# Decode attention beside an MLP: TensorE's loop over single (group, batch) pairs instead of two

## The chip, the cores and the metric

The kernel runs on one core of a Trainium2 chip. The metric is the device time of the program in microseconds (us). Every engine of the core runs its own instruction stream: TensorE (PE, with its weight loads shown as PEld), VectorE (DVE), ScalarE (ACT), GpSimd (POOL) and SyncE (SP), which here only issues transfers. They wait for each other by semaphores.

## The reference, cut to what matters

```python
def _A_ref(x, k_cache, v_cache, wq, wo):      # B=8, Sq=1, D=640, 32 heads, Sk=4096, Dh=128
    q = (x @ wq).reshape(B, Sq, Hq, Dh).transpose(0, 2, 1, 3)
    scores = jnp.einsum("bhqd,bhkd->bhqk", q, k_cache) * (Dh ** -0.5)
    o = jnp.einsum("bhqk,bhkd->bhqd", softmax(scores), v_cache)
    return o.transpose(0, 2, 1, 3).reshape(B, Sq, Hq * Dh) @ wo

def _B_ref(x, w1, b1, w2, b2):                # F=1728
    h = gelu(layernorm(x) @ w1 + b1)
    return h @ w2 + b2

xn = layernorm(x)
return x + _A_ref(xn, k_cache, v_cache, wq, wo) + _B_ref(xn, w1, b1, w2, b2)
```

All inputs are bfloat16. The K and V caches are 268 MB each, so nearly all that the kernel reads is cache.

## The kernel before, in words

The work is cut into 32 pairs i of a group of eight heads and one batch element. A pair's K is one transfer of 8.4 MB: partition (head, p) holds 256 consecutive keys of one head, 64 KB in a row. V has the same layout. K alternates between two slots (`kslot`), V has one slot (`VS`). SP issues in the order K(1), V(0), K(2), V(1), and so on; K(i) waits until K(i-2) has been worked off (`("kt", i-2)`, the last transposes and scores on TensorE's side, and `("km", i-2)`, the last VectorE chunk), and V(i) waits for the value product of pair i-1 (`("pv", i-1)`). An issue that waits holds up the ones behind it.

The scores of a pair come from two engines. TensorE takes `jp_of(i)` of the 256 keys of each partition, 128 for pair 0 and 80 for the others: `pe_T` transposes eight key blocks into one PSUM bank, `act_T` copies them to SBUF on ScalarE, `pe_QK` multiplies them with the query. VectorE takes the other keys in three chunks (`dve_chunk`: multiply by the broadcast query, add halves, reduce) and selects TensorE's scores with a mask (`dve_sel`). `dve_max` makes the maxima, `act_exp` eight exponentials, `pe_RS` the row sums, `pe_PV` the 256 products with V, `act_O` and `o_norm` the normalised output. `fin_wo` multiplies it with wo, in four parts (`WO_CUT`); wo lies in a K slot and its first two parts are multiplied between the products of pairs 30 and 31, the other two after that of pair 31. V of pair 31 comes in four pieces (`V_CUT`), each with a semaphore, and the product waits for each.

Nothing of this is scheduled by a compiler. Each step is given a position (`at(pos, fn, ...)`), the steps are recorded in the order of their positions, and each engine's list is replayed. Positions are 100 per pair: a pair's transposes and scores stand at 0 to 44, its exponentials at 90, its value product at 150, behind the transposes of the next pair. Only for pair 0 the exponentials stand at 145:

```python
at(o + 90 if i else o + Q + 45, act_exp, i)
at(o + Q + 48, pe_RS, i)
at(o + Q + 50, pe_PV, i)
```

To keep the program short, TensorE, VectorE and ScalarE replay the 15 equal stretches of two pairs from pair 2 on as a loop (`_replay_loop`), in which the value that a wait compares with grows with the loop's register. Pairs 0 and 1, the last product and wo are straight code around the loop. TensorE's loop head is put on the first slot of a block of instructions (`head_slot`).

The head of the program loads wq, w1, w2 and K(0), computes the queries and the whole MLP on TensorE (`pe_q`, `pe_mlp1`, `pe_mlp2`), and lets SP issue K(1) and V(0) after that.

Of the kernel before, what the change touches and what calls it, by code (L numbers as in the profile page):

```python
# [8 lines left out]
BF = mybir.dt.bfloat16  # L9
# [57 lines left out]

class _Dma:
# [26 lines left out]
def _emit(e, call, wait=None):  # L95
    name, a, k, inc = call
    if name == "wait_ge":
        e.wait_ge(a[0], a[1] if wait is None else wait, **k)
        return
    inst = getattr(e, name)(*a, **k)  # L100
    if inc is not None:
        inst.then_inc(*inc)
# [7 lines left out]
def _same(x):  # L110
    if hasattr(x, "ap") and hasattr(x, "offset"):
        return (x.tensor.name, x.offset, str(x.ap), str(x.dtype))
    return str(x)


def _replay_loop(e, calls, a, b, n, slot=None):

    size = (b - a) // n
    assert size * n == b - a and n >= 2
    _replay(e, calls[:a])  # L120
    body = calls[a:a + size]
    grow = []
    for j, (name, args, kw, inc) in enumerate(body):
        step = 0
        for r in range(1, n):
            name_r, args_r, kw_r, inc_r = calls[a + r * size + j]
            assert name_r == name and inc_r == inc and sorted(kw_r) == sorted(kw), (j, name, name_r)
            if name == "wait_ge":
                assert args_r[0] is args[0]
                if r == 1:  # L130
                    step = args_r[1] - args[1]
                assert args_r[1] == args[1] + r * step and args[1] > 0 and step >= 0, (j, args, args_r)
            else:
                assert [_same(x) for x in args_r] == [_same(x) for x in args], (j, name)
                assert [_same(kw_r[x]) for x in sorted(kw)] == [_same(kw[x]) for x in sorted(kw)], (j, name)
        grow.append(step)
    head = {} if slot is None else {"head_slot": {e.engine: slot}}
    with e.bass.Fori(0, n, engines=OrderedEngineSet([e.engine]), **head) as r:
        for call, step in zip(body, grow):
            _emit(e, call, call[1][1] + r * step if step else None)  # L140
    _replay(e, calls[b:])


def bass_parallel_sum__gqa_block_cached__mixer_channel_mlp__decode_kernel(
# [33 lines left out]
    V_CUT = (0, 96, 176, 232, 256)  # L178

    def jp_of(i):  # L180
        return 128 if i == 0 else 80
# [16 lines left out]
    with ExitStack() as es:  # L198
# [41 lines left out]
        qrep_sb = sb("qrep_sb", [P, 2, HS, HP], BF)  # L240
# [12 lines left out]
        rs_sb = sb("rs_sb", [P, 2, HS], F32)  # L253
        ri_sb = sb("ri_sb", [P, 2, HS], F32)
        ones_f = sb("ones_f", [P, P], F32)
        res_sb = sb("res_sb", [P, DC * B], BF)
# [12 lines left out]
        RS_ps = CH_ps[:, 384:384 + 2 * HS].rearrange("p (s h) -> p s h", h=HS)  # L269
# [3 lines left out]
        pe, dve, act, sp, pool = (_Eng(sem(f"{n}_s")) for n in ("pe", "dve", "act", "sp", "pool"))  # L273
        ld_s = [_Dma(sem(f"ld_s{s}")) for s in range(3)]
        ld_x, ld_b1, ld_b2, ld_wq, ld_w1, ld_w2a, ld_w2b, st_o = (
            _Dma(sem(n)) for n in ("ld_x", "ld_b1", "ld_b2", "ld_wq", "ld_w1", "ld_w2a", "ld_w2b", "st_o"))
        ld_vl = [_Dma(sem(f"ld_vl{q}")) for q in range(len(V_CUT) - 1)]
# [14 lines left out]
        def load_k(i):  # L292
            s = kslot(i)
            if i >= 2:
                sp.wait(tk[("kt", i - 2)], tk[("km", i - 2)])
            elif s == KB:
                sp.wait(tk["mlp"])
            tk[("k", i)] = ld_s[s].sig(sp.dma_start(tile[s], cache_src(A_k_cache, i)))

        def load_v(i):  # L300
            sp.wait(tk["mlp"] if i == 0 else tk[("pv", i - 1)])
            if i < NQ - 1:
                tk[("v", i)] = [ld_s[VS].sig(sp.dma_start(tile[VS], cache_src(A_v_cache, i)))]
                return
            tk[("v", i)] = [
                d.sig(sp.dma_start(tile[VS][:, lo:hi, :], cache_src(A_v_cache, i)[:, lo:hi, :]))
                for d, lo, hi in zip(ld_vl, V_CUT[:-1], V_CUT[1:])]

# [6 lines left out]
        def consts_pool():  # L315
            pool.iota(iota_h, [[-HP, HS]], base=0, channel_multiplier=1)
            tk["iota"] = pool.sig(pool.iota(iota_i, [[1, P]], base=0, channel_multiplier=-1))
            pool.memset(zeros_sb, 0.0)
            pool.memset(ones_sb, 1.0)
            pool.memset(mx_sb[:, :], 0.0)  # L320
            pool.memset(mb_sb[:, :], 0.0)
            tk["consts"] = pool.sig(pool.memset(ones_f[:, :], 1.0))
# [98 lines left out]
        def qrep(i):  # L421
            hq, b = divmod(i, B)
            s = i % 2
            pool.wait(tk["q"], tk.get(("qb_pe", i - 2)), tk.get(("qkl", i - 2)))
            tk[("qrep", i)] = pool.sig(pool.tensor_copy(
                qrep_sb[:, s, :, :],
                qT_sb[:, hq * HS:(hq + 1) * HS, b][:, :, None].to_broadcast([P, HS, HP])))

        def pe_qbc(i):
            pe.wait(tk[("qrep", i)], tk["id"])  # L430
            QBB.use(pe)
            tk[("qb_pe", i)] = QBB.used(pe, pe.sig(pe.matmul(
                QB_ps[:, 0:DH], qrep_sb[:, i % 2, :, :].rearrange("p h r -> p (h r)"),
                ident_bf[:, :], start=True, stop=True)))

        def act_qbc(i):
            act.wait(tk.get(("ym", i - 2)))
            QBB.use(act)
            tk[("qb", i)] = QBB.used(act, act.sig(act.activation(
                qbc_sb[:, i % 2, :], QB_ps[:, 0:DH], ACT.Copy)))  # L440

        def pe_T(i, t):
            n = group0[i] + t
            k = n % 2
            s = kslot(i)
            j0 = NKEY - jp_of(i) + t * TPB
            pe.wait(tk["id"], tk[("k", i)])
            TRB[k].use(pe)
            for jj in range(TPB):
                last = pe.transpose(TR_ps[:, k, jj * P:(jj + 1) * P], tile[s][:, j0 + jj, :], ident_bf[:, :])  # L450
            tk[("kt", i)] = TRB[k].used(pe, pe.sig(last))
# [13 lines left out]
        def pe_QK(i, t):  # L465
            n = group0[i] + t
            f = int(t >= halves(i)[1])
            t0 = halves(i)[f]
            pe.wait(tk[("ev", n)], tk[("qrep", i)])
            if t == t0:  # L470
                SBK[f].use(pe)
            for jj in range(TPB):
                c0 = ((t - t0) * TPB + jj) * HS
                last = pe.matmul(S_ps[:, f, c0:c0 + HS], KT_sb[:, n % NS, jj, :],
                                 qrep_sb[:, i % 2, :, 0], start=True, stop=True)
            tk[("qk", n)] = SBK[f].used(pe, pe.sig(last))
            tk[("qkl", i)] = tk[("qk", n)]

        def dve_chunk(i, c):
# [4 lines left out]
            dve.wait(tk[("k", i)], tk[("qb", i)])  # L484
# [40 lines left out]
        def act_exp(i):  # L525
            s = i % 2
            act.wait(tk[("nb", i)], tk.get(("pv", i - 1)), tk.get(("rs", i - 2)))
            for h in range(HS):
                last = act.activation(P_sb[:, h, :], Sd_sb[:, s, :], ACT.Exp, bias=NB_sb[:, s, h:h + 1],
                                      scale=SCALE, accum_out=rs_sb[:, s, h:h + 1])  # L530
            tk[("exp", i)] = act.sig(last)

        def pe_RS(i):
            s = i % 2
            pe.wait(tk[("exp", i)], tk["consts"])
            CHB.use(pe)
            tk[("rs", i)] = CHB.used(pe, pe.sig(pe.matmul(
                RS_ps[:, s, :], ones_f[:, :], rs_sb[:, s, :], start=True, stop=True)))

        def dve_rinv(i):  # L540
            CHB.use(dve)
            if i == NQ - 1:
                dve.wait(tk[("on", i - 2)])
            tk[("ri", i)] = CHB.used(dve, dve.sig(dve.reciprocal(ri_sb[:, i % 2, :], RS_ps[:, i % 2, :])))

        def pe_PV(i):
            PVB.use(pe)
            pe.wait(tk[("exp", i)])
            for j in range(NKEY):
                if j == 0 or (i == NQ - 1 and j in V_CUT):  # L550
                    pe.wait(tk[("v", i)][V_CUT.index(j)])
                last = pe.matmul(PV_ps[:, 0:HS], tile[VS][:, j, :], P_sb[:, :, j],
                                 start=(j == 0), stop=(j == NKEY - 1))
            tk[("pv", i)] = PVB.used(pe, pe.sig(last))

        def act_O(i):
            PVB.use(act)
            tk[("oU", i)] = PVB.used(act, act.sig(act.activation(oU_sb[:, i % 2, :], PV_ps[:, 0:HS], ACT.Copy)))

        def o_norm(i):  # L560
            hq, b = divmod(i, B)
# [59 lines left out]
        for i in range(NQ):  # L621
# [5 lines left out]
            at(o - 60, qrep, i)  # L627
# [14 lines left out]
            at(o + 90 if i else o + Q + 45, act_exp, i)  # L642
# [5 lines left out]
            at(o + Q + 75, o_norm, i)  # L648
        o = NQ * Q
# [4 lines left out]
        engs = {"pe": pe, "dve": dve, "act": act}  # L654
        marks = {n: [] for n in engs}
        for m in range(LOOPN + 1):
            for n in engs:
                at((LOOP0 + 2 * m) * Q - 12, lambda n=n: marks[n].append(len(engs[n].calls)))

# [3 lines left out]
        def replay(e, n):  # L663
            m = marks[n]
            assert len({y - x for x, y in zip(m, m[1:])}) == 1, (n, m)
            _replay_loop(e, engs[n].calls, m[0], m[-1], LOOPN, 0 if n == "pe" else None)
# [6 lines left out]
        def _(e):  # L673
            replay(e, "pe")
# [40 lines left out]
```

## Time and profile before

| what | value |
| --- | --- |
| median of 3 runs | 1288.85 us (1288.84 to 1289.09) |
| profiled execution | 1288.79 us, span 1287.0 us |
| bytes moved, mean rate | 552.15 MB, 429 GB/s |
| busy share of the span | PE 46%, PEld 41%, DVE 84%, ACT 36%, POOL 6% |
| mean granted TensorE clock | 0.619 |

The span runs from the first to the last instruction of the profiled execution; the rest of its own time lies around the span. Times inside the profile are counted from the span's start. A row of the timeline gives start, duration, engine, line, operation, result and operands with their shapes, the count, and in brackets the idle time before it with what ended it. A row of the chain gives start, duration and what the chain rests on there. A row of the windows gives the stretch, its length, the busy time and count of PE, PEld, DVE, ACT and POOL, the granted clock, the DMA share and GB/s. Nearly every instruction has line 100, since the recording layer issues them all there; tiles tell them apart: `TR_ps` transposed keys, `KT_sb` their copy, `S_ps` scores, `P_sb` exponentials, `CH_ps` row sums, `PV_ps` the value product, `ACC_ps` the sum of the outputs.

### The profile page before, as it was taken

How to read it: one execution, taken by the hardware profiler on the slowest of the kernel's cores; microseconds unless marked ns; L12 is line 12 of the kernel's file. 1: busy time of each engine (PE TensorE's matmuls, PEld its weight loads, DVE VectorE, ACT ScalarE, POOL GpSimd, SP SyncE). 2: the span in 40 equal slices, each digit the busy share in tenths (PEclk: the TensorE clock that was granted, in tenths of full speed). 3: DMA queues.
4: the chain of work that ended last, by engine and by line, in shares of the span. 5: the costliest groups of instructions: out<-in, count | busy, mean ns of one | idle time of the engine just before them, and what ended most of it. 6: DMA issues, size and time to landing. Idle time of an engine off the chain costs nothing.

```text
span 1287.0 us, 31562 instructions
## 1 busy us (share of the span) xinstructions
PE 590.6 (46%) x14000; PEld 527.9 (41%) x14000; DVE 1082.2 (84%) x662; ACT 468.4 (36%) x909; POOL 72.0 (6%) x74
## 2 busy tenths in 40 slices
PE   4454543553443453443453443553543553543554
PEld 4353443443443453443443443442433452433443
DVE  1599988988888988888988888988888988888982
ACT  1444432244432244432344432344432344422341
POOL 0001000000000000000000000000000000000000
PEclk9966555666655666656666655666556666656665
DMA  9999999999999999999999999999999999999998
GB/s 400 445 424 433 425 439 434 424 440 438 426 436 442 426 428 444 432 426 440 436 426 434 444 426 428 446 430 424 442 436 426 434 444 426 430 446 428 424 407 327
DMA packets 14413, 552.15 MB, mean 429 GB/s; under 512 B 1260, under 2 KB 5429, under 8 KB 5558
## 3 DMA queue, kind: packets, MB, share of 16 engines
q1 hardware_dynamic: 14320, 551.79, 99.5%
q8 instruction: 18, 0.29, 0.1%
q10 hardware_dynamic: 70, 0.03, 0.0%
q14 instruction: 5, 0.04, 0.0%
HBM read 551.80 MB, written 0.01 MB: 429 GB/s over the span
## 4 chain that ended last, share of the span: by engine, by line
DMA 78%; PE 17%; ACT 1%; DVE 1%; issue 1%; SPq 0%; another core or an unknown queue 0%; ACTq 0%
DMA S_sb<-in_A_v_cache_dram 75%; PE PV_ps L100 17%; DMA S_sb<-in_A_k_cache_dram 3%; ACT KT_sb L100 1%; DVE S_sb L100 1%; ACT P_sb L100 0%; DVE Sd_sb L100 0%; SPq L100 0%; PE TR_ps L100 0%; PE ACC_ps L100 0%; PE QB_ps L100 0%; PE S_ps L100 0%; DVE S_ps L100 0%; PE CH_ps L100 0%
## 5 line engine op out<-in xcount | busy, mean ns | idle before, releaser
L100 DVE TENSOR_TENSOR S_sb<-S_sb,qbc_sb 128x7552 bf16<-128x7552 bf16 (+3 forms) x96 | 385.6, 4016 | 149.1 <-DMA S_sb<-in_A_k_cache_dram 149.0
L100 PE MATMUL TR_ps<-ident_bf,S_sb 128*128 128x128 bf16 (+1 forms) x2618 | 260.5, 264 | 373.4 <-DMA S_sb<-in_A_k_cache_dram 365.9
L100 DVE TENSOR_REDUCE Sd_sb<-S_sb 128x59 f32<-128x3776 bf16 (+3 forms) x96 | 387.0, 4031 | 3.3
L100 PEld LDWEIGHTS TR_ps<-ident_bf,S_sb 128*128 128x128 bf16 (+1 forms) x2618 | 203.5, 119 | 379.3 <-DMA S_sb<-in_A_k_cache_dram 371.8
L100 ACT ACTIVATE KT_sb<-TR_ps 128x1024 bf16<-128x1024 bf16 x326 | 321.1, 1022 | 81.2 <-PE TR_ps L100 79.0
L100 PE MATMUL PV_ps<-P_sb,S_sb 128*128 128x8 bf16 x8192 | 225.1, 175 | 218.4 <-DMA S_sb<-in_A_v_cache_dram 208.2
L100 PEld LDWEIGHTS PV_ps<-P_sb,S_sb 128*128 128x128 bf16 x8192 | 221.5, 103 | 221.8 <-DMA S_sb<-in_A_v_cache_dram 211.5
L100 ACT ACTIVATE P_sb<-Sd_sb,NB_sb 128x256 bf16<-128x256 f32 x256 | 126.3, 494 | 230.3 <-DVE NB_sb L100 230.3
L100 DVE TENSOR_TENSOR S_sb<-S_sb 128x3776 bf16<-128x3776 bf16 (+3 forms) x96 | 201.4, 2098 | 3.3
L100 ACT ACTIVATE oU_sb<-PV_ps 128x8 f32<-128x8 f32 x31 | 5.5, 177 | 450.2 <-PE PV_ps L100 450.2
L100 PE MATMUL S_ps<-qrep_sb,KT_sb 128*128 128x8 bf16 x2608 | 123.8, 177 | 73.3 <-ACT KT_sb L100 61.5
L100 PEld LDWEIGHTS S_ps<-qrep_sb,KT_sb 128*128 128x128 bf16 x2608 | 95.2, 101 | 124.8 <-ACT KT_sb L100 87.3
L100 POOL TENSOR_TENSOR oT_sb<-oU_sb,ri_sb 128x8 bf16<-128x8 f32 x31 | 64.3, 2074 | 1122.3 <-ACT oU_sb L100 1089.4
L100 ACT ACTIVATION_READ_ACCUMULATOR P_sb<-Sd_sb,NB_sb 128x1 f32 x256 | 47.7, 186 | 0.0
L100 DVE TENSOR_REDUCE Sd_sb<-S_ps 128x40 f32<-128x320 f32 (+1 forms) x64 | 31.9, 498 | 2.2
L100 DVE TENSOR_TENSOR S_ps<-S_ps,mask_sb 128x320 f32<-128x320 f32 (+1 forms) x64 | 31.8, 496 | 1.5 <-PE S_ps L100 1.5
L100 PE MATMUL CH_ps<-rs_sb,ones_f 128*128 128x8 f32 x64 | 12.4, 266 | 12.1 <-ACT P_sb L100 12.1
L100 PEld LDWEIGHTS CH_ps<-rs_sb,ones_f 128*128 128x128 f32 x64 | 10.2, 201 | 12.3 <-ACT P_sb L100 12.3
L100 DVE TENSOR_REDUCE mx_sb<-Sd_sb 128x1 f32<-128x256 f32 x32 | 13.4, 420 | 1.1
L100 PE MATMUL CH_ps<-S_sb 128*128 128x8 bf16 (+1 forms) x244 | 12.0, 181 | 5.0 <-DMA S_sb<-in_A_wq_dram 4.4
L100 PEld LDWEIGHTS CH_ps<-S_sb 128*128 128x128 bf16 (+1 forms) x244 | 11.4, 120 | 5.7 <-DMA S_sb<-in_A_wq_dram 4.4
L100 ACT ACTIVATE qbc_sb<-QB_ps 128x128 bf16<-128x128 f32 x32 | 8.9, 277 | 11.8 <-PE QB_ps L100 9.9
(41 smaller groups left out, 87.7 us busy)
## 6 DMA issues: line engine op xcount, KB each, us to landing
S_sb<-in_A_wq_dram SPq DMA_DIRECT2D x1, 5120.0 KB, 15.2
S_sb<-in_A_v_cache_dram SPq DMA_DIRECT2D x1, 3072.0 KB, 12.8
S_sb<-in_A_wo_dram SPq DMA_DIRECT2D x1, 2560.0 KB, 32.4
S_sb<-in_A_v_cache_dram SPq DMA_DIRECT2D x1, 2560.0 KB, 20.0
S_sb<-in_B_w_dram SPq DMA_DIRECT2D x1, 2160.0 KB, 19.9
S_sb<-in_B_w_dram SPq DMA_DIRECT2D x1, 2080.0 KB, 25.7
S_sb<-in_A_v_cache_dram SPq DMA_DIRECT2D x1, 1792.0 KB, 23.8
S_sb<-in_A_wo_dram SPq DMA_DIRECT2D x1, 1280.0 KB, 35.6
```

Of the source, the lines that this page charges most:

```text
L100: inst = getattr(e, name)(*a, **k)
```

## The change

- TensorE's loop has 32 turns of one pair. Turn r holds the transposes and scores of pair r and the row sums and value product of pair r-1. Since K's slot alternates, each transpose takes its address from the loop's register (`_Slot`), which adds one register instruction a transpose.
- The last turn has no pair 32. A branch on the register (`If_lt`, `If_eq`) runs in its place the first two parts of wo, whose instructions stand in the loop's body and are jumped over in the other turns. The last value product is the loop's own; its waits for V's pieces stand in all turns and compare with 1 or, in the last turn, 17, and GpSimd sets these semaphores to 1 at the start. Behind the loop stand only the last two parts of wo and the store. `head_slot` is gone.
- So that all turns are alike: pair 0 takes 80 keys on TensorE like the others, its exponentials stand at 90 like the others (ahead of pair 1's evictions on ScalarE), some steps get a stand-in for pair -1 or 32, the repeated query and the row sums have one buffer instead of two, and TensorE waits for K through GpSimd (`k_ready`: a wait for the load, then a small memset that signals).
- K(0) comes in two transfers, keys 0 to 116 and 117 to 255; VectorE's first two chunks of pair 0 wait for the first.
- VectorE's and ScalarE's loops stay.

```diff
+class _Slot:
+    def __init__(self, slots, i, lo, n):
+        self.slots, self.i, self.lo, self.n = slots, i, lo, n
+    def at(self, i):
+        return self.slots[:, i % 2, self.lo:self.lo + self.n]
...
+def _replay_pe(e, calls, head, mid, end, late):
+    n = len(head)
+    first = [calls[a:b] for a, b in zip(head, mid)]
+    second = [calls[a:b] for a, b in zip(mid, head[1:] + [end])]
+    g1, g2 = _steps(first[:-1]), _steps([[c for c in t if not _late(c, late)] for t in second])
+    _replay(e, calls[:head[0]])
+    with e.bass.Fori(1, n + 1, engines=OrderedEngineSet([e.engine])) as r:
+        reg = e.to_reg(r)
+        with e.If_lt(reg, n):
+            for call, step in zip(first[0], g1):
+                _emit(e, call, call[1][1] + (r - 1) * step if step else None, r)
+        with e.If_eq(reg, n):
+            _replay(e, first[-1])
+        g = iter(g2)
+        for call in second[0]:
+            if _late(call, late):
+                e.wait_ge(call[1][0], (r >> (n.bit_length() - 1)) * 16 + 1)
+            else:
+                step = next(g)
+                _emit(e, call, call[1][1] + (r - 1) * step if step else None)
+    _replay(e, calls[end:])
...
+    K_CUT = (0, 117, 256)
     def jp_of(i):
-        return 128 if i == 0 else 80
+        return 80
...
-            tk[("k", i)] = ld_s[s].sig(sp.dma_start(tile[s], cache_src(A_k_cache, i)))
+            if i == 0:
+                lo, hi = K_CUT[0:2]
+                tk["k0"] = ld_k0.sig(sp.dma_start(tile[s][:, lo:hi, :], cache_src(A_k_cache, i)[:, lo:hi, :]))
+            lo, hi = K_CUT[1:3] if i == 0 else (0, NKEY)
+            tk[("k", i)] = ld_s[s].sig(sp.dma_start(tile[s][:, lo:hi, :], cache_src(A_k_cache, i)[:, lo:hi, :]))
...
+        def k_ready(i):
+            pool.wait(tk[("k", i)])
+            tk[("kr", i)] = pool.sig(pool.memset(kr_sb[:, :], 0.0))
...
         def pe_T(i, t):
-            pe.wait(tk["id"], tk[("k", i)])
+            pe.wait(tk["id"], tk[("kr", i)])
...
-                last = pe.transpose(TR_ps[:, k, jj * P:(jj + 1) * P], tile[s][:, j0 + jj, :], ident_bf[:, :])
+                last = pe.transpose(TR_ps[:, k, jj * P:(jj + 1) * P], _Slot(S_sb, i, (j0 + jj) * DH, DH),
+                                    ident_bf[:, :])
...
-            dve.wait(tk[("k", i)], tk[("qb", i)])
+            dve.wait(tk["k0"] if i == 0 and c < 2 else tk[("k", i)], tk[("qb", i)])
...
-            act.wait(tk[("nb", i)], tk.get(("pv", i - 1)), tk.get(("rs", i - 2)))
+            act.wait(tk[("nb", i)], tk.get(("pv", i - 1)))
...
-                if j == 0 or (i == NQ - 1 and j in V_CUT):
-                    pe.wait(tk[("v", i)][V_CUT.index(j)])
+                if j == 0:
+                    pe.wait(tk[("v", i)][0])
+                elif j in V_CUT:
+                    pe.wait_ge(ld_vl[V_CUT.index(j) - 1].sem, 1)
...
-            at(o - 60, qrep, i)
+            at(o - 52, qrep, i)
+            at(o - 2, k_ready, i)
...
-            at(o + 90 if i else o + Q + 45, act_exp, i)
+            at(o + 90, act_exp, i)
...
+        for i in range(1, NQ + 1):
+            at(i * Q - 12, mark, head)
+            at(i * Q + 47, mark, mid)
+        at(NQ * Q + 79, mark, end)
```

## The prediction

> **What bounds the kernel now.** I read the page's busy slices and queue table first, then the chain of waits in order of time, SP's timeline, TensorE's timeline at the head, and the windows of the tail.
>
> ```profile
> DMA  9999999999999999999999999999999999999998
> q1 hardware_dynamic: 14320, 551.79, 99.5%
> q8 instruction: 18, 0.29, 0.1%
> 1177.96 31.64 DMA S_sb<-in_A_v_cache_dram
> 1209.65 7.00 PE PV_ps L100 x256
> 1216.67 31.65 DMA S_sb<-in_A_v_cache_dram
> 1248.37 7.01 PE PV_ps L100 x256
> ```
>
> The DMA row is full from the second slice to the last but one: transfers bound the kernel. The chain looks like a loop of V load (31.6 us) and value product (7.0 us), 38.7 us a pair, but that is how the chain is followed back. One pair's K and V are 16.78 MB, and at the 433 to 434 GB/s that the windows give for a pair this is 38.7 us alone. V's 31.6 us hold 12.3 us of queueing behind K, so the product may end about 12 us later before an engine of the DMA runs dry; K is issued 25 us ahead.
>
> ```profile
> 74.06 0.33 SPq L100 DMA_DIRECT2D S_sb<-in_A_k_cache_dram  x1
> 96.21 0.33 SPq L100 DMA_DIRECT2D S_sb<-in_A_v_cache_dram  x1
> 85.79 6.39 PE L100 MATMUL PV_ps<-P_sb,S_sb 128*128 128x8 bf16 x233 [1.56 <-DMA S_sb<-in_A_v_cache_dram]
> 95.42 0.76 PE L100 MATMUL PV_ps<-P_sb,S_sb 128*128 128x8 bf16 x23 [3.24 <-issue]
> 128.61 3.58 PE L100 MATMUL PV_ps<-P_sb,S_sb 128*128 128x8 bf16 x128 [0.23 <-issue]
> 135.63 1.31 PE L100 MATMUL PV_ps<-P_sb,S_sb 128*128 128x8 bf16 x43 [3.43 <-issue]
> 1278.00:1280.00 2.00, 0.12 (x5) 0.02 (x1) 0.00 (x0) 0.00 (x0) 0.00 (x0) 0.50 0.75 287
> 1280.00:1282.00 2.00, 1.69 (x57) 1.60 (x58) 0.00 (x0) 0.00 (x0) 0.00 (x0) 0.50 0.39 141
> 1282.00:1284.00 2.00, 1.62 (x56) 1.56 (x57) 0.19 (x1) 0.00 (x0) 0.00 (x0) 0.50 0.07 20
> ```
>
> The products with "issue" in front stand still for up to 3.4 us with nothing to wait for, at boundaries 128 matmuls apart. A matmul is two instructions, so a block is 256, and each stop ends 1.3 us after a packet of the instruction queue (16,384 bytes, 18 in all). From one new block to the next such a burst needs 7.0 us (128.61 to 135.63), of which it computes 3.6.
>
> The last three rows show a ragged end: the DMA share falls from 0.75 to 0.07 over 4 us. The trace's packet records say why. A 64 KB packet takes 2.42 us and there are 16 such chains, one per engine. An instruction packet holds its engine 1.0 to 1.1 us, and the data packet behind it takes 2.9 instead of 2.42: about 1.5 us lost on that engine, which nothing gives back while all queues are full. The 16 completion marks of a load lie 0.5 us apart at 24.5 us, 2.0 at 65, 3.5 from 122 on. Fifteen of the 18 packets fall between 20 and 177 us, in turn on eight engines, so most of these carry two. At 1260, 1273 and 1281 us three more follow. The last V piece has its first mark at 1276.8 and its last at 1281.5 us, and the last piece of wo 1278.5 and 1283.16: the slowest engine is 4.7 us behind the fastest at the end.
>
> **The tail, changed.** In the built programs TensorE's code falls from 4,586 to 2,278 instructions; the loop is 1,190 instead of 1,709 and has only 85 behind it. With the block positions that the stall at product 233 fixes (63 instructions ahead of the program), the loop lies in blocks 4 to 8 and the tail ends in block 9. That leaves 8 instruction packets instead of 18, one to each of the eight engines, and none before the last V piece. If nothing else moved, engines with two packets would be one packet's 1.5 us earlier and those with three 3.0: the last V mark of a one-packet engine is 1280.0 - 1.5 = 1278.5 us against 1281.5, and the last mark of wo 1281.66 - 1.5 = 1280.2 against 1283.16. Behind them stand 24 products (0.8), the normalisation (0.2), 40 matmuls (1.2) and the store, unchanged. The loop's exit branch (76 ns) hides under the 0.34 us between the last product and the first wo matmul. Gain 3.0 us.
>
> **The steady turns.** 80 address computations a turn, one per transposed K block. TensorE's 75 fused register operations in the trace take 40 ns: 3.2 us a turn in its sequencer. K's score work of a pair now takes 11.8 us (609.77 to 621.56) and V lands at 629.1, so 7.5 us are free before the product moves at all, and 12.3 more before the DMA starves. Branches back take 208 ns, once a turn. GpSimd's new wait for K(i) has the next repeat of the query and the next normalisation queued behind it, and TensorE's transposes wait for its memset (0.1 us); the normalisation ahead of it is over 10 us before K lands (597.72 + 2.10 against 609.8), and the two behind it are needed only after this pair's scores and the next product, so K's landing still rules. The single buffers of query and row sums are free by then for the same reason. Nothing here; without the cover each turn would pay 3.2 us or more.
>
> **The head.** Three edits act here. K(0) in two pieces: VectorE starts with 117 keys, 139/256 of 19.4 us or 10.5 us earlier, at 36.4 instead of 46.97. It now has 176 keys rather than 128, by chunk rows of pair 2's kind 10.1, 10.3 and 10.3 us plus 1.9 for the selected scores. Chunks 0 and 1 end at 56.9, the second selection waits for TensorE until 59.2, chunk 2 ends at 70.6 (before: 74.0), and K(2), which waits for it, is issued 3.5 us earlier, under a queue that lasts to 83 us: worth nothing. 128 extra packets cost 8 ns each, eight to an engine: below 0.1 us.
>
> The exponentials of pair 0 now stand ahead of pair 1's evictions on ScalarE (before, behind them). They wait for the maxima (72.1) and take 4.0, so evictions that ran from 67.0 start at 76.1. TensorE's scores of pair 1 then end about 11.1 us later, at 87.2 (pair 2's row: 113.97 to 125.07, also started behind exponentials); before they ended at 78.7. Behind them on TensorE wait the row sums, V(0)'s product and, on SP, V(1)'s load. All of it is new code in the first turn. Block 6 is asked for when block 5 is entered, at the sixth transposed group (80.7), and is there 7.0 us later, 87.7. Take 88.0 for the jump over the wo branch into block 6; two more blocks at 7.0 us each and 102 products at 27 ns give 104.8 us for the end of V(0)'s product; it was 96.2.
>
> K(2)'s marks, the last work in the queues, run from 102.64 to 104.62. V(1) issued at 104.9 finds engines idle. The first packet comes 1.05 us after an issue (0.73 to 1.78 at the start), the last engine's up to 1.2 us after that. So all engines restart 3.3 to 4.4 us behind the fastest engine's schedule of before, and stay there, nearly level, since later instruction packets fall into the gap. I take 3.8.
>
> **Sum.** The slowest engine ends 3.8 instead of 4.7 us behind the same fastest one: 0.9 us gained, not 3.0. The profiled execution was 1288.79 us around a span of 1287.0, and the median is 1288.85: 1288.79 - 0.9 = 1287.9. The three runs agree within 0.25 us; 0.2% (2.6 us) is taken as no change.
>
> [...]
>
> **Rivals.** *No gap.* If a new block came in 5 us rather than 7, V(0)'s product ends at 100.8 and V(1) reaches the queues by 102: no engine waits, and the 3.0 us remain, 1285.8. For it: part of the 7 us is waiting for data packets of 2.42 us. Against it: three bursts of 6.7 to 7.0 us, and a cold branch of 7.02 us at 95.67.
>
> *Slower: the register addresses set the pace at the head.* No row shows a weight load whose address is in a register. Bounds: nothing, since 40 ns hide beside 76 ns a transpose, to about 85 ns each, the distance of a register operation from the load behind it (611.908 to 611.993), all of it in the open. A score group, 1.1 us now, would then take up to 1.8; pair 1's scores end at 94. From 1.2 us a group on the kernel is slower than before (the restart 0.9 us later). At 1.55 they end at 91.7, V(1) restarts 3.7 us later, 7.5 behind: 1288.8 + 2.8 = 1291.6. I took no delay, since TensorE's queue is fed ahead elsewhere; this end sets the range's top.
>
> *Every turn fetches its code again.* 31 turns of 5 packets on eight engines, 1.5 us each: 29 us, 1318. The loop of before, longer, ran from 177 to 1260 us without one packet, which speaks against it. [...]
>
> *The split and the shorter code do nothing at the end,* because the last V piece waits for something else: 1288.8. Against it are the marks.
>
> **How the numbers follow.** Small gap 0.45 (1286.4 to 1289.4, by 1.5 us either way of its restart); no gap 0.20; slow register addresses 0.20, of which 0.13 beyond 2.6 us; fetching every turn 0.05; nothing 0.10. Faster by over 0.2% is the second case, 0.20. Slower is 0.13 + 0.05 = 0.18. The rest, 0.62, is within. The range goes from the no-gap case (1285.7) to most of the slow one (1291.2); outside lie refetching, the worst addresses and some of the no-gap case.
>
> **What would show it.** Right: 8 packets on the instruction queue, none after 110 us before the last V piece; V(1) issued at 104 to 106 us with the DMA share below 0.9 around 104 to 106; the marks of a load nearly level from there on; 38.7 us a pair. Wrong: packets in every turn, V(1) before 102 with the share at 1.0 (no gap), or scores of pair 1 ending after 91 us.

## The result, and the profile after

The median after is 1290.34 us (22 runs, 1289.61 to 1293.13), against 1288.75 us before (22 runs): a ratio of 1.0018 with a 95% interval of 1.0011 to 1.0024. The change makes the kernel slower by 1.6 us, where 0.9 us of gain was forecast. The size is under the 0.2% that the prediction takes as no change, but the sign is clear: the fastest run after is slower than the slowest before. The profiled execution is 1290.35 us, 1.56 above that of before, so the two profiles show the difference that is to be explained. (The 22 times fall in two groups, 13 at 1289.6 to 1290.5 and 9 at 1292.0 to 1293.1; the profile belongs to the lower one.)

The page after, lines on the span, the DMA's busy slices and the queues:

```profile
span 1288.5 us, 34287 instructions
DMA  9998999999999999999999999999999999999998
q1 hardware_dynamic: 14464, 551.79, 99.4%
q8 instruction: 9, 0.15, 0.0%
```

The same bytes take 1.5 us longer, and the fourth slice (97 to 129 us) is no longer full. The instruction queue has 9 packets instead of 18: by the packet records at 21.6, 28.7, 51.9, 61.8, 86.0, 93.0, 100.5, 104.2 and, behind all the loads, 1285.4 us. The chain of waits, start, duration and what it rests on:

```profile
105.94 21.78 DMA S_sb<-in_A_v_cache_dram
127.77 7.04 PE PV_ps L111 x256
134.82 31.63 DMA S_sb<-in_A_v_cache_dram
166.50 7.04 PE PV_ps L111 x256
```

V(1)'s load takes 21.8 us here where the next one takes 31.6: there was no queue in front of it. From the second row on a pair takes 38.7 us, as before. TensorE's and SP's timelines at the head:

```profile
88.79 0.39 PE L111 MATMUL S_ps<-qrep_sb,KT_sb 128*128 128x8 bf16 x8 [0.86 <-ACT KT_sb L111]
89.96 0.90 PE L111 MATMUL PV_ps<-P_sb,S_sb 128*128 128x8 bf16 x28
95.49 3.57 PE L111 MATMUL PV_ps<-P_sb,S_sb 128*128 128x8 bf16 x128 [4.63 <-issue]
103.07 2.84 PE L111 MATMUL PV_ps<-P_sb,S_sb 128*128 128x8 bf16 x100 [4.01 <-issue]
105.94 0.33 SPq L111 DMA_DIRECT2D S_sb<-in_A_v_cache_dram  x1
```

The scores of pair 1 end at 89.18, V(0)'s product stands still twice for code, 4.63 and 4.01 us (each stop ends 1.4 to 1.5 us after a packet of the instruction queue does), and V(1) is issued at 105.94; before, at 96.21. The windows, DMA share in the last column but one, at the head and at the end:

```profile
102.00:104.00 2.00, 0.93 (x34) 0.93 (x35) 2.00 (x1) 0.00 (x0) 0.00 (x0) 0.50 0.15 66
104.00:106.00 2.00, 1.91 (x72) 1.82 (x69) 1.86 (x5) 0.05 (x1) 0.00 (x0) 0.50 0.03 8
1280.00:1282.00 2.00, 0.84 (x31) 0.85 (x32) 0.00 (x0) 0.00 (x0) 0.00 (x0) 0.50 0.97 390
1282.00:1284.00 2.00, 1.63 (x55) 1.45 (x52) 0.06 (x1) 0.00 (x0) 0.00 (x0) 0.50 0.77 266
1284.00:1286.00 2.00, 1.42 (x41) 1.26 (x41) 0.34 (x2) 0.00 (x0) 0.00 (x0) 0.50 0.04 10
```

For nearly 4 us next to nothing moves. At the end the share falls from 0.97 to 0.04 over two windows, where before it sank through 0.75, 0.39 and 0.07: the engines now end together. Their common end is late, though: V(1)'s 16 completion marks lie at 126.87 to 127.41 us (before 122.0 to 125.45), wo's last at 1284.15 (before 1283.16). What stands behind the loads is as before: the last V piece releases its 24 products at 1283.04 (before 1281.98), the normalisation and wo's last products follow, then the store's issue at 1286.42 (before 1285.30) and ScalarE's end.

### The profile page after: what moved, and what is told of

The parts are those of the page before. It is cut to its first block, busy times and chain, and to the rows that moved or that the text cites. A ratio compares the mean times of both kernels' runs of the same rounds, so it can differ in the third digit from the quotient of the medians.

```text
span 1288.5 us, 34287 instructions
## 1 busy us (share of the span) xinstructions
PE 672.9 (52%) x13904; PEld 573.5 (45%) x13904; DVE 1089.4 (85%) x663; ACT 475.4 (37%) x906; POOL 77.4 (6%) x107
## 4 chain that ended last, share of the span: by engine, by line
DMA 78%; PE 18%; ACT 1%; DVE 1%; issue 1%; SPq 0%; POOL 0%; ACTq 0%; DVEq 0%
DMA S_sb<-in_A_v_cache_dram 75%; PE PV_ps L111 17%; DMA S_sb<-in_A_k_cache_dram 3%; PE TR_ps L111 1%; ACT KT_sb L111 1%; DVE S_sb L111 0%; DVE Sd_sb L111 0%; PE S_ps L111 0%; ACT P_sb L111 0%; SPq L111 0%; PE ACC_ps L111 0%; PE CH_ps L111 0%; DVE S_ps L111 0%; DVE mx_sb L111 0%; PE QB_ps L111 0%
## 5 line engine op out<-in xcount | busy, mean ns | idle before, releaser
L111 PE MATMUL TR_ps<-ident_bf,S_sb 128*128 128x128 bf16 (+1 forms) x2570 | 339.9, 276 | 381.9 <-POOL kr_sb L111 367.4
L111 DVE TENSOR_TENSOR S_sb<-S_sb,qbc_sb 128x7552 bf16<-128x7552 bf16 (+1 forms) x96 | 388.8, 4050 | 143.7 <-DMA S_sb<-in_A_k_cache_dram 143.5
L111 PEld LDWEIGHTS TR_ps<-ident_bf,S_sb 128*128 (+2 forms) x2570 | 244.0, 103 | 439.4 <-issue 364.6
L111 DVE TENSOR_REDUCE Sd_sb<-S_sb 128x59 f32<-128x3776 bf16 (+1 forms) x96 | 390.2, 4065 | 3.3
L111 ACT ACTIVATE KT_sb<-TR_ps 128x1024 bf16<-128x1024 bf16 x320 | 326.9, 1023 | 124.1 <-PE TR_ps L111 112.6
L111 DVE TENSOR_TENSOR S_sb<-S_sb 128x3776 bf16<-128x3776 bf16 (+1 forms) x96 | 202.9, 2114 | 3.3
L111 PE MATMUL S_ps<-qrep_sb,KT_sb 128*128 128x8 bf16 x2560 | 122.0, 177 | 41.8 <-ACT KT_sb L111 38.3
L111 POOL TENSOR_TENSOR oT_sb<-oU_sb,ri_sb 128x8 bf16<-128x8 f32 x31 | 60.5, 1953 | 397.8 <-ACT oU_sb L111 381.2
L111 POOL COPY qrep_sb<-qT_sb 128x128 bf16<-128x128 bf16 x32 | 12.8, 399 | 461.1 <-PE S_ps L111 441.4
L111 DVE TENSOR_REDUCE Sd_sb<-S_ps 128x40 f32<-128x320 f32 x64 | 31.5, 492 | 2.2
L111 DVE TENSOR_TENSOR S_ps<-S_ps,mask_sb 128x320 f32<-128x320 f32 x64 | 31.4, 490 | 1.7 <-PE S_ps L111 1.7
```

## The experiments

The theory: the time is that of the DMA engine that is last; all engines restart with V(1) after the gap, so the time follows V(1)'s issue; V(1) is late through cold code in the loop's first turn. Cold is a block of 256 instructions that TensorE runs for the first time, warm one that has run. The profile before shows both. Counted in TensorE's records, back from the stop at product 233 and, in the loop, on from its first instruction at 102.75 us (the stops at 135.62 and 172.47 are its instructions 768 and 1,536), each of the 15 blocks entered first between 18 and 173 us is followed by one packet of 16,384 bytes, 2.8 to 5.0 us later (95.42 by that at 100.23, 128.61 by that at 132.99, 135.62 by that at 140.64); products that reach the next block sooner stand still, for up to 3.43 us. From 177 to 1260 us, where the loop's code has run, there is no such packet. The rivals: the steady turns or the slower transposes cost the time, instruction packets are worth nothing, or the loop as such makes the gap.

**A first turn that only branches.** TensorE's loop starts at 0; the turn with register 0 skips every section, so that the blocks are touched in idle time.

```diff
-    with e.bass.Fori(1, n + 1, engines=OrderedEngineSet([e.engine])) as r:
+    with e.bass.Fori(0, n + 1, engines=OrderedEngineSet([e.engine])) as r:
...
+        u = (r + (n - 1)) & (n - 1)          # in place of r - 1 in the waits
+        with e.If_ne(reg, 0):                # around both sections of the turn
```

> The changed kernel with one more turn of TensorE's loop ahead of the others, in which every section is jumped over: its branches only touch blocks 5, 6 and 8 of the code while TensorE would wait for K(1) and the exponentials anyway (59 to 76 us). Theory (the slowest DMA engine sets the end; the cold value product of pair 0 makes a gap in the queues): the product then runs in 7.1 us without the stops of 4.6 and 4.0 us, V(1) is issued before 101 us instead of 105.94, the DMA share has no hole at 104 to 107, each engine carries one instruction packet at most, and the time is about 1285.8 us (1285.3 to 1287). Rival (the packets and the ragged end do not matter, only the gap does): 1288.8 us, as before the change. Rival (the time is lost in the turns or in the tail): 1290 us, unchanged.

Measured: 1292.39 us (7 runs), 1.0029 of before, 1.0018 to 1.0040. The timelines of this kernel:

```profile
81.61 0.28 PE L111 MATMUL QB_ps<-ident_bf,qrep_sb 128*128 128x128 bf16 x1 [21.85 <-issue]
100.97 6.98 PE L111 MATMUL PV_ps<-P_sb,S_sb 128*128 128x8 bf16 x256
107.97 0.33 SPq L111 DMA_DIRECT2D S_sb<-in_A_v_cache_dram  x1
```

The product is warm, 6.98 us without a stop. But three branches to cold blocks took 4.8, 7.0 and 8.7 us and ended only at 80.3, and the query's broadcast of pair 1, which stands behind them on TensorE, came at 81.61; ScalarE's copy of it has the exponentials behind it, so evictions began 11 us later. I had not counted what is queued behind the branches. V(1) went out 2.03 us later than in the changed kernel, its slowest mark came 2.04 later (129.45), the last mark of wo 2.25 later (1286.40), and the time is 2.05 longer. The cure failed, the rule that the time follows V(1) held.

**The same with two blocks only.** The branching turn touches only the two blocks that the product needs, and the broadcast stands ahead of the loop.

```diff
+    m = [c[0] for c in first[0]].index("matmul") + 1
+    _replay(e, first[0][:m])                 # the broadcast of pair 1, ahead of the loop
...
-    with e.bass.Fori(1, n + 1, engines=OrderedEngineSet([e.engine])) as r:
+    with e.bass.Fori(0, n + 1, engines=OrderedEngineSet([e.engine])) as r:
...
+        with e.If_ne(reg, 0):
+            with e.If_lt(reg, n):
+                with e.If_ne(reg, 1):        # the broadcast
```

> The changed kernel with a first turn of TensorE's loop that only branches, from block 4 to 6 and on to 8, and with the query broadcast of pair 1 issued ahead of the loop, so that ScalarE's exponentials of pair 0 need not wait for that turn. Theory (the end is the slowest DMA engine; the cold product makes the gap): the branches end between 75 and 80 us, the scores of pair 1 between 89 and 94, the value product of pair 0 runs without a stop and V(1) is issued between 97 and 101.6 us, so no queue runs dry; the marks of V(1) run from 122.0 to 124 us, 8 instruction packets in all, the last mark of V(31) near 1278.8 and the time 1286.4 us (1286.0 to 1287.2), which beats both kernels. Rival (the packets and the ragged end do not matter): 1288.8. Rival (something in the turns costs the time): 1290.

Measured: 1287.97 us (11 runs), 0.9993, 0.9984 to 1.0002. The timelines of this kernel:

```profile
92.21 6.98 PE L111 MATMUL PV_ps<-P_sb,S_sb 128*128 128x8 bf16 x256
99.22 0.33 SPq L111 DMA_DIRECT2D S_sb<-in_A_v_cache_dram  x1
```

The product ran without a stop, V(1) was issued at 99.22 and queued behind K(2); no gap. The time is 2.4 us below the changed kernel, but it can't be told from the kernel before, and it is 1.6 over what was expected. Two instruction packets lay in flight together, at 71.3 and 71.5 us, and took 1607 and 2191 ns instead of some 1050. Followed from each packet's end to the next one's start, the records put them on two engines, and these come out 1.0 and 1.4 us behind the others (V(1)'s marks 121.94 to 123.91, then 124.89 and 125.31). The last marks of wo show the same two steps (1281.08 and 1281.52, the others by 1280.14).

**More gap.** The changed kernel with K(0) in one transfer.

```diff
-            if i == 0:
-                lo, hi = K_CUT[0:2]
-                tk["k0"] = ld_k0.sig(sp.dma_start(tile[s][:, lo:hi, :], cache_src(A_k_cache, i)[:, lo:hi, :]))
...
-            dve.wait(tk["k0"] if i == 0 and c < 2 else tk[("k", i)], tk[("qb", i)])
+            dve.wait(tk[("k", i)], tk[("qb", i)])
```

> The changed kernel with K(0) in one transfer again. Theory: VectorE starts at 47.0 instead of 36.4 us, the maxima, exponentials, scores of pair 1 and the cold product behind them come 10 us later, V(1) is issued near 116 us, and the gap grows by 10 us: 1299 to 1301 us. Rival (the early start is hidden by other waits): 1290 us.

Measured: 1296.14 us (5 runs), 1.0058, 1.0044 to 1.0072. V(1) was issued at 111.49, 5.55 us later than in the changed kernel, its slowest mark came 5.53 later (132.94) and the time is 5.80 longer. V(1) was late by less than the 10 expected, since the cold blocks came faster once the queues were running empty: the packets lie at 102.6, 106.3 and 110.3, some 4 us apart instead of 7. So the split of K(0) is worth 5.8 us in this kernel.

**Turn 1 as straight code, pair 0's exponentials behind the evictions as before.**

```diff
-    with e.bass.Fori(1, n + 1, engines=OrderedEngineSet([e.engine])) as r:
+    with e.bass.Fori(2, n + 1, engines=OrderedEngineSet([e.engine])) as r:   # pair 2 on
...
-            at(o + 90, act_exp, i)
+            at(o + 90 if i else o + Q + 45, act_exp, i)   # a stand-in signals at 90
```

> The changed kernel with the first turn of TensorE's loop as straight code ahead of it, and the exponentials of pair 0 behind pair 1's evictions again (a stand-in keeps ScalarE's count). Theory: scores of pair 1 end near 79 us as before the change, the value product of pair 0 is still cold but ends near 96 us, V(1) is issued there and there is no gap; 11 or 12 instruction packets by 180 us give four engines two and four engines one, so the slowest is some 3.4 us behind the fastest instead of 4.7: 1287.6 us (1287 to 1288.4). Rival (packets do not matter): 1288.8. Rival (the register addresses or the branches of the turns cost it): 1290.

Measured: 1291.79 us (8 runs), 1.0022, 1.0012 to 1.0033. V(1) was issued at 97.10 and had no gap, but the loop's first turn, now pair 2's, was as cold. The timelines of this kernel:

```profile
131.50 0.59 PE L111 MATMUL CH_ps<-rs_sb,ones_f 128*128 128x8 f32 x2 [7.47 <-issue]
145.47 0.39 PE L111 MATMUL PV_ps<-P_sb,S_sb 128*128 128x8 bf16 x9 [3.17 <-issue]
145.89 0.33 SPq L111 DMA_DIRECT2D S_sb<-in_A_v_cache_dram  x1
```

A jump over wo of 7.47 us, then cold products, and V(2) issued at 145.89 under queues that ran dry from 141.47 to 145.02. The gap moved by a pair, and the last mark of wo is at 1286.04, 1.9 us behind the changed kernel's. Pair 0's exponentials alone are therefore not the cause of a gap.

**wo and the last product out of the loop.** 31 turns without branches; the last product and the first parts of wo stand straight behind the loop.

```diff
-    with e.bass.Fori(1, n + 1, engines=OrderedEngineSet([e.engine])) as r:
-        with e.If_lt(reg, n):
...
-        with e.If_eq(reg, n):
-            _replay(e, first[-1])
+    with e.bass.Fori(1, n, engines=OrderedEngineSet([e.engine])) as r:
...
+    _replay(e, first[-1])
+    for call in second[-1]:
+        _emit(e, call, 17 if _late(call, late) else None)
```

> The changed kernel with 31 turns and no branches: the last value product and the first two parts of wo stand behind the loop again, as straight code. Theory: the gap at the head stays as it is (V(1) issued near 106 us), and 3 instruction packets come back at the tail, after 1255 us, two of them ahead of the last V marks: one engine ends 0.6 to 1.5 us later than in the changed kernel, which makes 1290.9 to 1291.8 us where the changed kernel has 1290.3 on the same chip. Rival (packets at the tail are hidden): the same as the changed kernel.

Measured: 1287.84 us (11 runs), 0.9994, 0.9985 to 1.0003. I had expected the gap to stay. The timelines of this kernel:

```profile
89.65 0.76 PE L111 MATMUL PV_ps<-P_sb,S_sb 128*128 128x8 bf16 x23
90.77 3.58 PE L111 MATMUL PV_ps<-P_sb,S_sb 128*128 128x8 bf16 x128 [0.36 <-issue]
98.06 2.97 PE L111 MATMUL PV_ps<-P_sb,S_sb 128*128 128x8 bf16 x105 [3.71 <-issue]
101.06 0.33 SPq L111 DMA_DIRECT2D S_sb<-in_A_v_cache_dram  x1
```

One long stop instead of two. The wo section is 243 instructions, nearly a block, and lay between the scores and the product. My reading, which no record of this kernel shows directly: the jump over it left no time for the packet behind. In the changed kernel that jump ends at 89.26 us in the product's first block, whose 28 products are over at 90.86, and the next packet starts at 93.00, 3.7 us after the entry. Without the jump V(1) is issued at 101.06 and queues behind K(2). What it cost: three packets are back in the tail (1258.0, 1271.4, 1278.8), and three engines end at 1280.85, 1281.31 and 1281.56 where all others end by 1280.04.

**wo first in the turn.** The last step, with one pair of sections swapped, so that nothing has to be moved out of the loop:

```diff
-        with e.If_lt(reg, n):
-            for call, step in zip(first[0], g1):
-                _emit(e, call, call[1][1] + (r - 1) * step if step else None, r)
         with e.If_eq(reg, n):
             _replay(e, first[-1])
+        with e.If_lt(reg, n):
+            for call, step in zip(first[0], g1):
+                _emit(e, call, call[1][1] + (r - 1) * step if step else None, r)
```

> The wo section of TensorE's loop stands ahead of the section with pair r's scores, so the first turn jumps over it while TensorE waits for pair 0's last work at 59 to 66 us, and nothing is jumped over between the scores of pair 1 and V(0)'s product; code, loop and tail are otherwise those of the changed kernel. Theory (wo's place in the body makes the gap; packets of instructions at the end cost their engines 1.5 us each): products of V(0) as 28, 128 without a stop, 100 behind one of 3.7 us, V(1) issued at 100.7 instead of 105.94 and not late for the queues; last V mark 1278.8, no packet in the tail; 1286.4. That is 1.4 below the kernel with wo behind the loop (1287.84), which has the same start and three packets in its tail. Rival one (packets at the end are worth nothing): the same start, 1287.8 or more. Rival two (the gap is not from wo's place but from the loop as such): V(1) again at 105 to 106, time 1290.3.

Measured: 1286.47 us (11 runs, 1286.23 to 1287.30), 0.9984 of before, 0.9975 to 0.9993: the fastest of all, 0.07 from the theory's number, though less than 0.2% below the kernel before. Its timelines, then its windows at the end:

```profile
89.99 4.35 PE L111 MATMUL PV_ps<-P_sb,S_sb 128*128 128x8 bf16 x156
98.35 2.84 PE L111 MATMUL PV_ps<-P_sb,S_sb 128*128 128x8 bf16 x100 [4.01 <-issue]
101.22 0.33 SPq L111 DMA_DIRECT2D S_sb<-in_A_v_cache_dram  x1
```

```profile
1278.00:1280.00 2.00, 1.70 (x63) 1.60 (x61) 0.00 (x0) 0.00 (x0) 0.00 (x0) 0.50 0.87 317
1280.00:1282.00 2.00, 1.56 (x60) 1.50 (x58) 0.19 (x1) 0.00 (x0) 0.00 (x0) 0.50 0.08 28
```

The jump over wo is still cold, 4553 ns, but it falls at 59.67 us, when TensorE has nothing to do. 28 and 128 products follow each other without a stop, one stop of 4.01 remains, V(1) is issued 4.72 us earlier than in the changed kernel and the DMA has no gap. Eight packets lie ahead of the last data, none in the tail, and the last wo mark is at 1280.80. This settles both halves: with pair 0's exponentials where the change has them, wo's place in the turn decides whether there is a gap, and without the gap the change is a gain. Against the version with wo behind the loop, which starts alike, the missing tail packets are worth 0.76 us at the last mark, 0.87 between the profiled executions and 1.4 between the medians (1.2 when each is taken against the kernel before in its own group of runs, 1288.79 and 1288.64).

**Are the transposes slower, and does it matter?** A group of eight transposes and eight scores takes longer in the changed kernel: by the starts of ScalarE's evictions 1.25 us at the head (76.42 to 87.71, nine steps) and 1.22 in a steady turn, before 1.13 and 1.03. Two kernels let the transposes read the identity at a fixed address, so that TensorE's share of the scores holds no keys, and keep every block of code behind the section in its place with 80 instructions that wait for something long there: ahead of the section in the first kernel (its page counts 34,287 instructions, as the changed kernel's does), one ahead of each transpose in the second.

```diff
         with e.If_lt(reg, n):
+            for _ in range(160):             # first kernel only; two waits to an instruction
+                e.wait_ge(late[0], 1)
             for call, step in zip(first[0], g1):
+                if call[0] == "transpose":   # second kernel only, in place of the lines above
+                    e.wait_ge(late[0], 1)
+                    e.wait_ge(late[0], 1)
...
-  pe.transpose(TR_ps[...], _Slot(S_sb, i, (j0 + jj) * DH, DH), ident_bf[:, :])
+  pe.transpose(TR_ps[...], ident_bf[:, :], ident_bf[:, :])
```

> The changed kernel, but the 80 transposes of a pair in TensorE's loop read the identity at a fixed address instead of K at an address from a register (so TensorE's share of the scores is wrong), and 80 instructions with waits that are long fulfilled stand ahead of the section in place of the 80 register operations, so every block of code behind the section lies as before. In the changed kernel a group of eight transposes and eight scores takes 1.25 us at the head and 1.22 in the steady turns (evictions 76.42 to 87.71 and 613.58 to 624.53, nine steps); in the kernel before 1.13 and 1.03 (67.00 to 77.21 and 610.85 to 620.11). Theory (the register address makes the groups slower, and the end of pair 1's scores sets the gap): 1.03 to 1.13 us a group, scores of pair 1 end near 87.6 instead of 89.18, V(1) issued at 104.3 to 104.6 instead of 105.94 and its slowest mark 1.3 to 1.6 us earlier; 1288.8 against 1290.3. Rival (the groups are slower through something else, such as the new wait through GpSimd, or the gap does not follow the scores): V(1) at 105.9 and 1290.3.

> As the kernel with the fixed address, but each of the 80 instructions with a fulfilled wait stands right ahead of its transpose, where the changed kernel has the register operation (TensorE's share of the scores is wrong here too). If the address from a register is what makes a group slower: 1.03 to 1.13 us a group and a time near 1288.8. If any further instruction between two transposes does: 1.2 us or more a group and 1290.3.

Measured: the first 1290.32 us (11 runs), 1.0012, 1.0003 to 1.0021; the second 1292.28 (9 runs, 1290.05 to 1292.80), 1.0025, 1.0015 to 1.0035. Groups: first kernel 1.18 us at the head (76.16 to 86.81) and 1.07 in a steady turn (613.60 to 623.23); second 1.25 (76.19 to 87.44) and 1.21 (614.29 to 625.15). These single turns ran at different granted clocks, though: between 613 and 625 us it is 0.50 in the changed kernel, 0.93 before, 0.78 in the first of the two and 0.65 in the second. Taken over all pairs from 180 us on and sorted by the clock granted during their groups, a group takes:

| granted clock | before | fixed address, waits ahead | fixed address, waits between | changed |
| --- | --- | --- | --- | --- |
| 0.6 to 0.7 | 1.12 us | 1.10 us | 1.21 us | 1.21 us |
| 0.7 to 0.8 | 1.08 us | 1.05 us | 1.21 us | 1.20 us |

So it is not the address from a register: a long fulfilled wait in the same place costs as much. At a like clock the instruction ahead of each transpose makes a group 0.09 to 0.15 us slower, about 11 to 19 ns each; the rest of the step from 1.03 to 1.22 goes with the clock. And it does not matter. The first kernel's timelines:

```profile
88.90 0.90 PE L111 MATMUL PV_ps<-P_sb,S_sb 128*128 128x8 bf16 x28
95.37 3.56 PE L111 MATMUL PV_ps<-P_sb,S_sb 128*128 128x8 bf16 x128 [5.57 <-issue]
103.22 2.84 PE L111 MATMUL PV_ps<-P_sb,S_sb 128*128 128x8 bf16 x100 [4.29 <-issue]
```

The product began 1.06 us earlier than in the changed kernel, and stood still just so much longer: the next two blocks came as there (packets at 93.0 and 100.8 against 93.0 and 100.5), V(1) was issued at 106.09, and the time is the changed kernel's. My theory's number, 1288.8, was missed: reaching the section earlier did not bring the blocks earlier. The block ahead of these came 2.5 us earlier (83.5 against 86.0), one data packet's 2.42 us. The records, followed engine by engine where the queues are full, show why steps of this size come about: every instruction packet starts within 0.1 us of the end of a data packet on its engine, so it moves by whole data packets or not at all.

**Does a packet in the tail always cost?** The kernel before with 14 turns of its loop instead of 15, so that more straight code stands behind it.

```diff
-    LOOP0, LOOPN = 2, 15
+    LOOP0, LOOPN = 2, 14
```

> The kernel before with 14 instead of 15 turns of its two-pair loops: the same work, with two more pairs as straight code behind the loops. Theory: 6 to 7 more instruction packets between 1180 and 1260 us, one more for nearly every one of the eight engines, 1.5 us more lag at the end: 1290.2 us (1289.6 to 1291). Rival (packets are hidden): 1288.8 us.

Measured: 1289.60 us (11 runs), 1.0008, 0.9999 to 1.0017, which by itself decides nothing. The profiled execution, 1290.37, is one of the three slowest of the 11, so it can't say why the other eight, 1289.23 to 1289.80, came in below the expected 1290.2. It shows two things. Seven more packets after 1197 us spread a load's marks to 4.97 us (before 3.37). But the code also made V(31) late and the engines more level again (its first piece 1268.23 to 1270.83), and the last mark of wo came at 1284.72, 1.56 us later than before. A gap late in the run took back part of what packets had spread; how much of the 1.56 is the gap is open.

**The changed kernel again,** three more times, for the two groups in its times.

> The changed kernel once more, unchanged, as the base of this call and for its two levels: 13 of 22 runs lay between 1289.6 and 1290.5 us and 9 between 1292.0 and 1293.1. If the upper level is a block of instructions that comes one data packet (2.42 us) later in the first turn, a profile of it shows V(1) issued near 108.3 us instead of 105.9, and all that follows 2.3 us later. If it is something else, V(1) is issued near 106 us in both.

> The changed kernel once more, for one profile. Its timed runs fall at 1289.6 to 1290.7 and at 1292.0 to 1293.1. If the upper level is a cold block that arrives one data packet (2.42 us) later in the first turn, a profile in it shows V(1) issued near 108.3 and all marks 2.4 us later; a profile in the lower level shows 105.9 to 106.1 again.

> As the run before it: a profile in the upper level (time about 1292.5) shows V(1) issued near 108.3 if a late block makes it, and 105.9 to 106.1 if something later in the run does.

Measured: 1290.65 us (11 runs: seven at 1289.65 to 1290.69, four at 1292.30 to 1292.66), 1.0017, 1.0008 to 1.0026; single runs of 1290.24 and 1290.54. All three profiles fell in the lower group (V(1) issued at 106.14, 106.08 and 105.63), so the upper one stays unexplained. The kernel with waits between the transposes gives one hint: its profile, at 1290.88, has V(1)'s marks within 0.3 us of the changed kernel's, but data packets of up to 2.67 us between 132 and 148 us instead of 2.42 (the changed kernel: up to 2.43), and the next load ends 0.6 us later on all engines. The last of these three profiles has such packets too (up to 2.67 us at 141 and 156 us): V(1)'s marks lie 0.35 to 0.45 us ahead of the changed kernel's, and V(2)'s 0.4 to 0.7 behind. What makes them slow is not known.

## Why the prediction was wrong, step by step

**The mechanism** was right: the transfers bind, the ragged end goes, and the late V(1) gives back what the tail gains. There are 8 packets before the last V piece and none after 110 us, as stated; V(1) is issued between 104 and 106 with the DMA share at 0.03; V(1)'s marks are level to 0.54 us. A gain was forecast and a loss came, because one term was too small.

**The failed step is the restart,** "I take 3.8". V(1)'s slowest mark is 5.4 us behind the old fastest schedule (127.41 against 122.0), which is more than the 4.7 of the ragged end that it replaces. Three parts. The cold blocks: 7.5 us from the assumed 88.0 to the first restart and 7.58 from there to the second, where 7.0 was taken for each, so V(1) was issued at 105.94 instead of 104.9. The choice in the range: 3.3 to 4.4 was worked out for first and last engine, and the middle was taken, although the slowest sets the end. And a term that was not in the sum: the first 64 KB packets into the empty queues take 2.6 to 3.35 us instead of 2.42 (3.1 on average). Added up: 3.8, plus 1.0 for the later issue, less 0.3 because the first packets came 1.2 us after the issue on average where 3.8 holds 1.5, plus 0.7 for the slow first packets, plus 0.25 from the average engine to the slowest, is 5.4.

**The end.** 5.4 at the head became 5.65 at the last mark of wo (1284.15 against the old fastest 1278.5): the spread grew from 0.5 to 1.15 us by two 8 KB instruction packets of other engines (523.8 and 954.4). So 1.89 of the miss of 2.46 between the profiled executions (1290.35 against 1287.89) lie in the DMA: the last mark was forecast at 1282.26. Another 0.13 lies in the steps from the last mark to the store, 0.35 in ScalarE's own end, where 0.75 us lie between its last branch and the span's end instead of 0.39, and 0.09 outside the span (not so in the other three profiles of this kernel, which have 1.81 us there, as before). ScalarE's 0.35 was a term at nothing; it is in all the variants of the changed kernel but the one with turn 1 as straight code, and why is open.

**The steady turns** cost nothing, as stated and for the reason stated: the 7.5 us of slack took it, and a pair stayed at 38.7 us. What was wrong is the lower bound of the rival, taken at the head as well, that 40 ns hide beside a transpose: the further instructions made a group 0.09 to 0.15 us slower at a like clock, a pair's ten up to 1.5 us.

**The slow register addresses** were a rival at 0.20, and its threshold ("from 1.2 us a group on") was crossed, at 1.25. Yet its sign, scores of pair 1 that end after 91 us, did not come (89.18), and the fixed address brought no gain, so the loss came out on this rival's side for another reason. That TensorE's queue is fed ahead, the ground for "no delay", can be read before from one register instruction: it ran at 609.84 us, when two of the eight transposes that stand ahead of it had started (609.77 and 609.79).

**No gap** was the rival at 1285.8. Its condition, a block in 5 us instead of 7, did not come true; its outcome did by one swap of sections, at 1286.47, where the packets are still 7.1 to 7.6 us apart (88.2, 95.8 and 102.9): in the order of the change the first turn needs three cold blocks after 80 us, with wo ahead of the scores two. The 3.0 us for the tail come out as 2.2 of measured gain (1288.64 for the kernel before in the same runs), with ScalarE's 0.35 already paid.

**Fetching every turn** did not come true: between the packets at 104.2 and 1285.4 us the queue of the 16,384-byte packets has none, and 31 turns ran in that time.

**K(0) in two pieces** started VectorE at 36.3 us, where 36.4 was worked out. Only K(2)'s earlier issue was priced, at nothing; what the earlier exponentials are worth where V(1) is late, 5.8 us, was not.

## What to carry to other kernels

Where transfers bind, look at the slowest DMA engine's last completion, and ask of any change to the code when new blocks are first entered and which load waits behind them: in this kernel 243 instructions that do not run in the first turn cost 3.9 us by lying between two parts that do. Put a section that is jumped over where its engine idles anyway. And a gap in the queues sets back all engines for the rest of the run (5.4 us here), while an instruction packet under full queues sets back one engine, by some 1.5 us as an estimate from the packets (1.0 to 1.1 us for the packet itself and 0.5 for the data packet behind it).

## What the runs showed of the hardware that was not expected

- Restarting empty queues cost twice, for V(1) in the changed kernel: 0.96 us from the issue to the first packet, then 2.6 to 3.35 us for first packets that otherwise take 2.42.
- Packets of cold blocks lay 7.0 to 7.6 us apart under full queues in the first turn (86.0, 93.0 and 100.5 in the changed kernel), and some 4 us when the queues were empty (102.6, 106.3 and 110.3 with K(0) in one transfer).
- Under full queues an instruction packet starts within 0.1 us of the end of a data packet on its engine. In the kernel that reached the product 1.06 us earlier, one packet lay 2.5 us earlier (83.5 against 86.0), and the next stayed at 93.0.
- Two instruction packets in flight together, on different engines (71.3 and 71.5 us, branching turn with two blocks), took 1.6 and 2.2 us instead of some 1.05.
- Taken branches to cold code took 4.8 to 8.7 us with the branching turn and 4.6 with wo first; those back to the head of the loop, over code that had run, 0.21 in the changed kernel.
- An instruction ahead of each of eight transposes, even a wait long fulfilled, made their group 0.09 to 0.15 us slower at a granted clock of 0.6 to 0.8.
